# A fused attention and two feed-forward layers on one core: another order of the same 1776 steps

## The chip, the core and the metric

One core of one Trainium2 chip. The metric is the device time of one execution in microseconds (us), lower is better. The engines are TensorE (PE, its weight loads shown as PEld), VectorE (DVE), ScalarE (ACT), GpSimd (POOL) and SyncE (SP, which here only issues DMAs). Each engine runs its own instructions strictly in the order in which the program lists them.

## What is computed

```python
scores = scale * np.matmul(q, k.transpose(0, 1, 3, 2))        # 2 x 12 heads, 448 x 448, head size 64
scores = np.where(mask, -1000000000.0, scores)                # causal
attn = np.exp(scores - np.max(scores, axis=-1, keepdims=True))
attn = attn / (np.sum(attn, axis=-1, keepdims=True) + 1e-09)
x = np.matmul(attn, v)                                        # then laid out as 896 tokens x 768
h = x @ w_in; r = np.maximum(h, 0.0); x = (r * r) @ w_out     # 768 -> 2048 -> 768
h = np.maximum(np.maximum(x @ w1, x @ w2), x @ w3)            # three times 768 -> 768
return h @ w_o                                                # 768 -> 768
```

All inputs and outputs are float32.

## The kernel before

The work has two parts that overlap a little. First comes the attention, for 12 pairs of heads. Behind it come four products of the feed-forward layers, each done by Strassen-like sevens: seven products M1 to M7 of sums of halves instead of eight, with each operand split into a high and a low part so that three matmuls (high by high, low by high, high by low) make one product.

The order of everything is written out by hand in one string, ORDER (line 28), of 1776 step names. A loop at the end walks through it and calls each step, and each step issues its instructions at once, on the engines that it names. So ORDER fixes for every engine what stands behind what; only semaphores between the engines decide when something starts. After the string's end a fixed piece of code finishes the last product.

The steps of the attention, for pair number i (the number behind the dot): `s0`, `s2`, `s4`, `s6` are score matmuls on PE; `m0` to `m6` subtract, mask and find the extreme on DVE (line 474); `e0` to `e6` are the exponentials on ACT (482); `a0` to `a2` and `r0` to `r2` add the small constant and take the reciprocal of the sums (489, 493); `n0` to `n6` multiply by it (497; the tiles 0 and 1 are 128 wide, 2 and 3 are 256, 4 and 5 are 384, 6 is 448); `g0` to `g3` transpose on PE (508); `h0` to `h3` copy the transposed probabilities to where the last product wants them (521 for `h3`, 523 for the others: `h0` 768 wide, `h1` and `h3` 512, `h2` 256); `w0` to `w3` are the last product on PE (533), which needs all four `h` of its pair. `xf`, `xh`, `xl` copy the result out (540, 544, 203); `d1` to `d4`, `1h` to `4h` and `1l` to `4l` make sums of results and split them.

The steps of the layers: the block of weights `i4` is loaded by SP into one of two buffers, `C.i4` makes a cast of its upper half (264 or 267), `J.i4` joins the two halves on DVE (274) and issues the next load. `T1` to `T4` make the sums of weight blocks (213, on DVE; for `w_out` three of the four are accumulating DMAs that POOL issues, 210). `H.f0M6` casts the high part of the weights for product M6 of the seven f0 (200 on ACT, 290 on POOL), `L.f0M6` subtracts it to get the low part on DVE (203), `M6.f0` runs its 9 or 10 matmuls on PE (605), and `V0.f0M6` and so on read the result out of PSUM on ACT and DVE. Letters f, o and h stand for the three groups of sevens: w_in, w_out, and w1 to w3. The high and low parts lie in a ring of 5 buffers.

A step name with an apostrophe is the same step on another engine: `H'` and `C'` are POOL's in place of ACT's, `h'`, `xh'` and `xf'` DVE's in place of ACT's, `n'` DVE's in place of POOL's, `a'` POOL's in place of DVE's, `1h'` to `4h'` POOL's in place of ACT's. For blocks of w_out the apostrophe of `C'` has no effect.

```python
for n in ORDER.split():
    todo[n]()
    step, *i = n.split(".")
    if step == "s0" and int(i[0]) + 3 < B * NP:
        todo[f"load.{int(i[0]) + 3}"]()
```

Of the kernel before, what the change touches and what calls it, by code (L numbers as in the profile page):

```python
# [33 lines left out]
n3.1 n5.2 n2.1 e0.2 s4.3 e1.2 s2.3 g1.1 a2'.2 e3.2 n6.2 w1.0 m4.3 e1.3 n4.2 w2.0 e0.3 h1.1 a1'.2
m5.3 m2.3 m3.3 e4.3 r2.2 r1.2 n0.2 g3.1 m6.3 e5.3 a2'.3 h3.1 g0.2 g3.2 w3.0 n3'.2 h0.2 xh'.0 h3.2
xf'.0 n2.2 s6.4 r2.3 g1.2 s2.4 h1.2 e2.3 s0.4 n1.2 xl.0 e3.3 m2.4 a1'.3 m3.4 e6.3 a0'.3 g2.2 m1.4
h2.2 w0.1 e3.4 m6.4 m0.4 e2.4 s4.4 r1.3 n2'.3 s2.5 n3.3 a1'.4 r0.3 e6.4 m4.4 m5.4 n1.3 g1.3 w1.1
n0'.3 m2.5 m3.5 n6'.3 w2.1 w3.1 n5.3 e1.4 r1.4 e0.4 n4.3 e5.4 e4.4 a2'.4 e3.5 s6.5 g2.3 h1'.3
h2'.3 g3.3 m6.5 d3.1 h3.3 s4.5 g0.3 m4.5 s0.5 C'.i0 e2.5 h0.3 n2.4 w0.2 n3.4 a0'.4 3h'.1 w1.2 r2.4
m1.5 w2.2 r0.4 e6.5 e4.5 e1.5 m5.5 n0'.4 m0.5 n1.4 e0.5 a1.5 w3.2 n6.4 xf.2 r1.5 g1.4 g2.4 J.i0  # L40
n5.4 g3.4 s6.6 h1'.4 h2.4 s2.6 a2.5 n4.4 3l.1 r2.5 h3.4 m2.6 n2.5 e5.5 m3.6 xh.2 e2.6 a0'.5 xl.2
r0.5 s4.6 g0.4 n3.5 e3.6 a1'.6 h0.4 m5.6 e5.6 s0.6 m0.6 w0.3 m1.6 w1.3 w2.3 n6.5 w3.3 m4.6 n0.5
n1.5 g3.5 m6.6 e0.6 e1.6 r1.6 e6.6 d2.3 xh.3 g1.5 n5.5 h3'.5 g2.5 h2'.5 h1.5 s6.7 n4.5 m6.7 g0.5
e4.6 a2'.6 a0'.6 n3.6 xl.3 s2.7 d1.3 m3.7 h0.5 n2.6 e6.7 s4.7 s0.7 r0.6 C'.i2 1h.3 m2.7 m0.7 r2.6
m5.7 e3.7 e2.7 w0.4 w1.4 m1.7 n0.6 w2.4 w3.4 n1.6 e1.7 e5.7 a1'.7 n5.6 m4.7 d4.3 s0.8 g2.6 e4.7
xh.4 n4'.6 g1.6 xf.4 r1.7 a0'.7 h1.6 n6.6 s6.8 m1.8 e1.8 m0.8 s2.8 h2'.6 s4.8 r0.7 n6.7 1l.3 g3.6
m2.8 e0.8 m3.8 2h'.3 xl.4 g0.6 H'.f0M1 a2'.8 w0.5 e0.7 4h'.3 m4.8 w1.5 e2.8 e3.8 w2.5 h3.6 m5.8
n5'.7 w3.5 g3.7 n4'.7 s4.9 a2'.7 r2.7 a1.8 n3.7 m6.8 n1.7 e4.8 h0.6 r1.8 n2.7 g0.7 J.i2 h3.7 g1.7
d3.5 e6.8 m5.9 s6.9 w0.6 m4.9 e5.8 n0.7 h0.7 g2.7 m6.9 s2.9 3h'.5 h1.7 e4.9 2l.3 m2.9 H'.f1M2 e6.9
s0.9 w1.6 m3.9 w2.6 h2.7 H'.f1M1 a0'.8 3l.5 w3.6 n2.8 n3.8 g1.8 e5.9 r0.8 L.f1M2 xh.6 n6.8 a0.9  # L50
m0.9 s2.10 n4.8 m1.9 n5.8 s6.10 r2.8 s4.10 h1.8 r0.9 m3.10 xf.6 e3.9 xl.6 n6.9 C'.i1 n1.8 g0.8
# [6 lines left out]
T1.f0 h1.10 r2.11 a0'.11 r0.11 h0.10 2h.7 g3.10 w1.9 n4'.11 w2.9 w3.9 h3.10 n6'.11 n1.11 n5.11
e3.11 M2a.f0 n0'.11 g0.11 d3.9 g2.11 e2.11 w0.10 w1.10 T2.f0 a1.11 r1.11 w2.10 h0.11 C.i4 w3.10
4l.3 n2.11 h2'.11 g3.11 n3.11 3h.9 d4.7 H'.f0M6 2l.7 T3.f1 3l.9 h3.11 xh.10 g1.11 h1.11 xl.10  # L60
H'.f0M5 M2b.f0 xf.10 L.f0M6 J.i4 T3.f0 T4.f0 M1a.f1 M1b.f1 M1c.f1 1h'.7 1l.7 w0.11 C.i5 w1.11
4h'.7 w2.11 V0.f1M1 V0.f0M1 J.i5 w3.11 more 4l.7 d2.11 T2.f1 M2c.f0 H.f1M6 2h'.11 M2a.f1 M2b.f1
H'.f1M3 2l.11 M2c.f1 C.i7 L.f1M6 M6.f0 H.f0M7 L.f0M5 V0.f0M6 M6.f1 d1.11 J.i7 1h.11 H.f1M5 L.f0M7
C.i11 L.f1M5 wload d4.11 M7.f0 H.f1M7 xh.11 1l.11 V0.f0M7 H'.f0M4 T4.f1 4h.11 M5.f1 xl.11 T1.f2
V0.f1M6 V0.f0M2 M5.f0 L.f0M4 J.i11 C.i6 M4.f0 V1.f0M7 L.f1M7 M7.f1 H.f1M4 H.f2M1 J.i6 L.f2M1
V0.f0M4 T1.f3 H'.f0M3 H.f3M5 T2.f2 V0.f1M7 V0.f1M2 L.f0M3 L.f1M4 M1.f2 V1.f1M2 C.i10 L.f1M3 T2.f3
L.f3M5 M4.f1 H.f3M1 L.f3M1 V2.f0M7 V2.f1M2 V0.f1M4 V0.f2M1 4l.11 M3.f0 H'.f2M6 J.i10 C.i12 V1.f1M7
M1.f3 M3.f1 V0.f3M1 H'.f3M6 V3.f0M7 T3.f3 J.i12 T1.f5 H.f3M7 L.f3M6 H.f2M2 M6.f3 H.f3M2 C'.i13
L.f2M6 V0.f1M3 L.f2M2 M2.f2 T4.f2 L.f3M2 V0.f0M3 J.i13 V2.f1M7 C.i8 H'.f2M5 L.f2M5 T3.f2 V0.f3M6
L.f3M7 T4.f3 M5.f3 M2.f3 V0.f3M2 M6.f2 H.f2M7 J.i8 T3.f5 H.f2M4 V0.f2M6 M7.f3 L.f2M7 L.f2M4 C'.i9  # L70
J.i9 H'.f3M4 M7.f2 V0.f3M7 L.f3M4 M5.f2 M4.f3 T1.f4 V0.f2M2 V1.f3M7 C'.o3l J.o3l H.f5M1 L.f5M1
T1.f6 T2.f6 V0.f2M7 H.f3M3 T2.f5 T3.f4 H'.f4M1 L.f4M1 V1.f0M4 V0.f3M4 H.f5M6 XH.o1M1 C.i15 M4.f2
V1.f2M7 V0.f2M4 T2.f4 L.f5M6 H'.f2M3 M1.f5 L.f3M3 V3.f1M7 V0.f5M1 V2.f2M7 M1.f4 L.f2M3 H'.f4M6
L.f4M6 V0.f4M1 J.i15 M3.f2 H.f4M2 L.f4M2 C.i14 V0.f2M3 V1.f3M4 J.i14 H'.f5M5 V1.f2M4 M6.f4 T1.f7
H.f5M2 V1.f1M4 S3.o1 T4.f5 C'.o0l M6.f5 V0.f4M6 M2.f4 L.f5M2 H'.f4M7 J.o0l H'.f5M7 V1.f0M2 M2.f5
# [1180 lines left out]
```

## Time and profile before

| what | value |
|---|---|
| time, median of 3 runs | 445.79 us (444.44 to 446.27) |
| the profiled execution's own time | 446.14 us |
| its span | 444.4 us |
| granted TensorE clock, mean share | 0.999 |
| busy in the span: PE, DVE, ACT, POOL | 98%, 90%, 65%, 37% |

The span is the profiled execution from its first to its last instruction; its own time adds 1.7 us around that. The busy share of PE says little by itself, because matmuls overlap and their ends are modelled: it is the stretches of time that tell which engine sets the pace.

### The profile page before, as it was taken

How to read it: one execution, taken by the hardware profiler on the slowest of the kernel's cores; microseconds unless marked ns; L12 is line 12 of the kernel's file. 1: busy time of each engine (PE TensorE's matmuls, PEld its weight loads, DVE VectorE, ACT ScalarE, POOL GpSimd, SP SyncE). 2: the span in 40 equal slices, each digit the busy share in tenths (PEclk: the TensorE clock that was granted, in tenths of full speed). 3: DMA queues.
4: the chain of work that ended last, by engine and by line, in shares of the span. 5: the costliest groups of instructions: out<-in, count | busy, mean ns of one | idle time of the engine just before them, and what ended most of it. 6: DMA issues, size and time to landing. Idle time of an engine off the chain costs nothing.

```text
span 444.4 us, 7641 instructions
## 1 busy us (share of the span) xinstructions
...
## 2 busy tenths in 40 slices
...
GB/s 241 213 126 195 189 174 113 135 165 189 164 139 210 140 143 147 227 192 214 149 90 153 248 75 142 71 143 71 164 121 214 144 140 3 0 1 0 45 45 160
DMA packets 42854, 61.04 MB, mean 137 GB/s; under 512 B 2112, under 2 KB 35008, under 8 KB 42816
## 3 DMA queue, kind: packets, MB, share of 16 engines
...
q14 instruction: 18, 0.15, 0.1%
...
## 4 chain that ended last, share of the span: by engine, by line
PE 47%; DVE 2%; DMA 2%; ACT 0%; issue 0%
PE ps L605 38%; PE ps L1045 7%; DMA wr<-in_moe_w 2%; PE ps L1152 1%; DVE wd L274 0%; DVE g L213 0%; DVE wq L203 0%; DVE y L213 0%; ACT up L264 0%; DVE s L213 0%; DVE x L834 0%; ACT wq L200 0%; ACT x L827 0%; ACT y L887 0%; DVE x L203 0%
## 5 line engine op out<-in xcount | busy, mean ns | idle before, releaser
L605 PE MATMUL ps<-s,wq 128*128 128x448 f32 (+1 forms) x629 | 130.4, 361 | 0.0
L605 PEld LDWEIGHTS ps<-s,wq 128*128 128x128 f32 x629 | 115.5, 188 | 9.6 <-DVE s L203 0.4
L605 PE MATMUL ps<-x,wq 128*128 128x448 f32 (+1 forms) x518 | 104.6, 362 | 0.6 <-DVE wq L203 0.4
L605 PEld LDWEIGHTS ps<-x,wq 128*128 128x128 f32 x518 | 94.6, 188 | 9.9 <-DVE wq L203 1.6
L605 PE MATMUL ps<-a,wq 128*128 128x448 f32 x459 | 99.5, 367 | 0.0
L605 PEld LDWEIGHTS ps<-a,wq 128*128 128x128 f32 x459 | 86.0, 188 | 7.3 <-issue 0.3
L290 POOL CAST wq<-wd 128x384 fp32r<-128x384 f32 x43 | 46.9, 1092 | 85.9 <-PE ps L605 82.8
L203 DVE TENSOR_TENSOR wq<-wd,wq 128x384 fp32r<-128x384 f32 x99 | 57.4, 593 | 5.6 <-POOL wq L290 3.0
L274 DVE SCALAR_TENSOR_TENSOR wd<-wr,up 128x768 int32<-128x768 int32 x56 | 56.0, 999 | 6.3 <-ACT up L267 2.5
L290 POOL CAST wq<-wt 128x384 fp32r<-128x384 f32 x35 | 28.0, 801 | 88.9 <-PE ps L605 71.2
L482 ACT ACTIVATE pr<-pr,st 128x256 f32<-128x256 f32 (+3 forms) x84 | 44.0, 532 | 3.7 <-DVE st L474 3.0
L203 DVE TENSOR_TENSOR wq<-wt,wq 128x384 fp32r<-128x384 f32 x68 | 39.4, 588 | 7.3 <-POOL wq L290 6.3
L264 ACT CAST up<-wr 128x768 f16<-128x768 bf16 x28 | 30.3, 1081 | 21.4 <-DVE wd L274 15.9
L497 POOL TENSOR_SCALAR pr<-pr,st 128x128 f32<-128x128 f32 (+3 forms) x68 | 40.7, 611 | 8.5 <-DVE st L493 6.1
L200 ACT CAST wq<-wd 128x384 fp32r<-128x384 f32 x56 | 28.5, 511 | 19.1 <-PE ps L605 17.8
L200 ACT CAST wq<-wt 128x384 fp32r<-128x384 f32 x33 | 16.8, 511 | 22.7 <-PE ps L605 18.9
L474 DVE CUSTOM_DVE_ANT_0 pr<-pp,mask 128x256 f32<-128x256 f32 (+2 forms) x72 | 27.5, 413 | 4.2 <-PE pp L463 3.9
L639 ACT COPY s<-ps 128x448 f32<-128x448 f32 x38 | 20.0, 530 | 16.5 <-PE ps L605 16.5
L508 PEld LDWEIGHTS pp<-ident,pr 64*128 64x128 f32 x384 | 15.4, 138 | 14.2 <-POOL pr L497 5.8
L203 DVE TENSOR_TENSOR x<-g,x 128x448 fp32r<-128x448 f32 x40 | 25.2, 645 | 1.4 <-ACT x L200 1.4
L200 ACT CAST x<-g 128x448 fp32r<-128x448 f32 x40 | 22.1, 563 | 5.3 <-PE ps L605 2.5
L533 PE MATMUL ps<-ph,v 128*64 128x448 f32 (+3 forms) x192 | 24.5, 389 | 0.1
...
## 6 DMA issues: line engine op xcount, KB each, us to landing
...
```

Source lines behind the costliest of these rows:

```text
L200: nc.scalar.copy(hi, src)
L203: nc.vector.tensor_tensor(out=lo, in0=src, in1=hi.bitcast(F32), op=SUB)
L264: copy(self.up.bitcast(FH)[:, :, 1::2], self.top)
L274: nc.vector.scalar_tensor_tensor(out=self.t.bitcast(I32), in0=self.rest, scalar=13, in1=self.up.bitcast(I32), op0=ALU.logical_shift_right, ...
L290: copy(self.t[:, 0], self.src())
L474: nc.vector.tensor_tensor_reduce(out=self.pr[:, offs[u]:offs[u] + n], in0=self.sc[u][:, :n], in1=mask[:, mask.shape[1] - n:], scale=-SCALE ...
L482: nc.scalar.activation(sl, sl, ACTF.Exp, bias=self.st[:, 0, u:u + 1], scale=-1.0, accum_out=self.st[:, 1, u:u + 1],)
L497: engine.tensor_scalar(sl, sl, self.st[:, 2, u:u + 1], 1.0, op0=ALU.mult, op1=ALU.mult)
L533: nc.tensor.matmul(self.pv[r, kc * P:], self.n["v"][:, kc, r], self.ph[:, h, at], start=kc == 0, stop=kc == NK - 1,)
L605: nc.tensor.matmul(acc[:, c], w, x[:, c], skip_group_check=True, **flags)
L639: nc.scalar.copy(self.s[n], self.b)
L1045: nc.tensor.matmul(acc, a, b, start=start and i == 0 and e == 0, stop=i == KH - 1 and e == 2, skip_group_check=True,)
```

## The change

The string ORDER is replaced by another order of the same steps. Ahead of the apostrophes the two lists hold the same 1776 names. 161 steps change their engine: among them 49 casts `H` go from POOL to ACT and 30 the other way, so that POOL has 61 of them now instead of 80; DVE has 13 of the 48 copies `h` of the placed probabilities, not 10 (three more `h1`, one more `h3`, one less `h2`), 18 products `n` for 16 (eleven 128 wide, not five; two 384 wide, not five; one 448 wide, not two), 11 additions `a` for 10, and no `xf` for 1. The two calls that start a load ahead of its turn (`wload`) stand elsewhere: the first stood in pair 0 and stands in pair 1, the second stood behind `C.i11` and stands behind `L.f7M7`. The new string is one line shorter, so every later line number is less by one. Nothing else is touched.

```diff
 ORDER = """
-s2.0 m2.0 m3.0 s0.0 m1.0 e2.0 s4.0 m0.0 e3.0 e0.0 m4.0 s6.0 e1.0 a1'.0 s2.1 wload e4.0 s0.1 m5.0
+s2.0 s0.0 m2.0 s4.0 m0.0 m1.0 s6.0 e2.0 e1.0 m3.0 m4.0 s2.1 e3.0 m5.0 s0.1 m6.0 a1'.0 e4.0 e5.0
...
```

DVE at the end of the attention, ahead of the first product that needs a sum of weights. Before, from the reciprocal of pair 11 (`r1.11`, on st_1080) over the copy `h2'.11` (ph_1255) to `L.f0M6`, the last row:

```order
L493 RECIPROCAL st_1080<-st_1080 128x2
L203 TENSOR_TENSOR s4_827<-s_748,s4_827 128x448
L523 COPY ph_1255<-pp4_73 128x2x2x64
L213 TENSOR_TENSOR s_1274<-s_966,s_1076 128x448
L203 TENSOR_TENSOR s2_1195<-s_1076,s2_1195 128x448
L213 TENSOR_TENSOR wt_1279<-wd_1123 128x384
L203 TENSOR_TENSOR s3_1272<-s_1239,s3_1272 128x448
L203 TENSOR_TENSOR a12_1283<-ps7_69,a12_1283 128x448
L203 TENSOR_TENSOR wq_1276<-wt_1188,wq_1276 128x384
```

Now, from behind the copy `h1'.11` to the same `L.f0M6` (wq_1294, the last row):

```order
L273 SCALAR_TENSOR_TENSOR wd_1289<-wr_1134,up_64 128x768
L212 TENSOR_TENSOR wt_1311<-wd_983 128x384
L202 TENSOR_TENSOR s2_1097<-s_1032,s2_1097 128x448
L202 TENSOR_TENSOR a12_1300<-ps7_69,a12_1300 128x448
L212 TENSOR_TENSOR wt_1311<-wd_537,wt_1198 128x384
L212 TENSOR_TENSOR wt_1339<-wd_1132 128x384
L273 SCALAR_TENSOR_TENSOR wd_1341<-wr_1291,up_64 128x768
L202 TENSOR_TENSOR wq_1322<-wt_1311,wq_1322 128x384
L202 TENSOR_TENSOR s1_1155<-s_1091,s1_1155 128x448
L202 TENSOR_TENSOR s4_1336<-s_1201,s4_1336 128x448
L212 TENSOR_TENSOR s_1362<-ps7_69,s_1218 128x448
L202 TENSOR_TENSOR wq_1294<-wt_1198,wq_1294 128x384
```

Between the last copy of a placed probability and `L.f0M6` stood 5 instructions on DVE, and 11 stand there now. In all of DVE's program ahead of `L.f0M6` the steps outside the attention proper are eight more: two joins `J`, three sums `T`, one `L`, one sum `d` and, net, one `l`.

PE at the same place. Before, the last product of pair 10 ends (ps7_69, first row), 16 transposes of pair 11 follow, 12 matmuls of M2.f0 and M1.f1, the last product of pair 11, 12 matmuls more, and M6.f0 (wq_1276):

```order
L533 MATMUL ps7_69<-ph_1171,v_1102 64x64 x2
L508 MATMUL pp2_77<-ident_90,pr1_109 128x64 x8
...
L605 MATMUL ps0_1221<-a12_946,wq_1150 128x448 x3
L605 MATMUL ps2_1314<-a11_391,wq_927 128x448 x3
...
L533 MATMUL ps7_69<-ph_1255,v_1154 64x448 x2
...
L605 MATMUL ps0_1221<-a12_1283,wq_1150 128x448 x3
L605 MATMUL ps3_1315<-a12_600,wq_916 128x448 x3
...
L605 MATMUL ps6_68<-s2_804,wq_1276 128x448 x3
```

Now (M6.f0 is wq_1294):

```order
L532 MATMUL ps7_69<-ph_1153,v_1080 64x448 x2
L507 MATMUL pp2_77<-ident_90,pr1_109 128x64 x8
L507 MATMUL pp4_73<-ident_90,pr1_109 128x64 x4
L532 MATMUL ps7_69<-ph_1153,v_1080 64x320 x2
...
L604 MATMUL ps2_1306<-a11_348,wq_826 128x448 x3
...
L532 MATMUL ps7_69<-ph_1266,v_1164 64x448 x2
...
L604 MATMUL ps3_1307<-a12_1300,wq_800 128x448 x3
L604 MATMUL ps0_1224<-a12_1300,wq_1043 128x448 x3
L604 MATMUL ps6_68<-s2_696,wq_1294 128x448 x3
```

The transposes now stand inside pair 10's last product; 30 matmuls of the layer stand ahead of pair 11's last product instead of 24, and 6 behind it instead of 12. Ahead of M6.f0 there are 36 in both.

## Rows read from the trace of the kernel before

**Rows 1.** Busy time by stretch: engine busy (instructions), clock, DMA share, GB/s.

```profile
60.00:80.00 20.00, 18.13 (x198) 12.04 (x195) 19.51 (x61) 17.46 (x48) 15.23 (x25) 1.00 0.39 111
95.00:215.00 120.00, 120.00 (x601) 110.89 (x600) 107.41 (x184) 92.63 (x190) 41.40 (x43) 1.00 0.66 175
```

Behind the stretch's length the busy times stand in this order: PE, PEld, DVE, ACT, POOL.

**Rows 2.** Timeline of PE, 78 to 93 us: start, length, what.

```profile
78.80 2.69 PE L605 MATMUL ps<-a,wq 128*128 128x448 f32 x12
81.42 1.95 PE L533 MATMUL ps<-ph,v 128*64 128x448 f32 x16
...
85.84 7.38 PE L605 MATMUL ps<-s,wq 128*128 128x448 f32 x35
```

**Rows 3.** Timeline of DVE, 74 to 87 us, around the end of the attention.

```profile
76.67 0.42 DVE L523 COPY ph<-pp 128x256 f32<-128x256 f32 x1
...
80.12 0.83 DVE L203 TENSOR_TENSOR wq<-wt,wq 128x384 fp32r<-128x384 f32 x1
```

**Rows 4.** Groups on DVE, 0 to 95 us: count, busy, mean ns, idle before.

```profile
L274 DVE SCALAR_TENSOR_TENSOR wd<-wr,up 128x768 int32<-128x768 int32 x8 | 8.3, 1035 | 0.0
L203 DVE TENSOR_TENSOR s<-s,s 128x448 fp32r<-128x448 f32 x11 | 7.5, 686 | 0.5 <-POOL s L559 0.5
...
L203 DVE TENSOR_TENSOR wq<-wt,wq 128x384 fp32r<-128x384 f32 x6 | 3.4, 593 | 0.0
L213 DVE TENSOR_TENSOR wt<-wd 128x384 f32<-128x384 f32 x5 | 3.3, 654 | 0.0
...
L497 DVE TENSOR_SCALAR pr<-pr,st 128x384 f32<-128x384 f32 x5 | 2.5, 521 | 0.0
L213 DVE TENSOR_TENSOR wt<-wd,wt 128x384 f32<-128x384 f32 x4 | 2.2, 547 | 0.0
L523 DVE COPY ph<-pp 128x256 f32<-128x256 f32 x5 | 2.1, 416 | 0.2 <-PE pp L508 0.2
...
L489 DVE TENSOR_SCALAR st<-st 128x2 f32<-128x2 f32 x8 | 1.9, 253 | 0.1
L213 DVE TENSOR_TENSOR s<-ps,s 128x448 f32<-128x448 f32 x3 | 1.9, 617 | 0.0
...
L497 DVE TENSOR_SCALAR pr<-pr,st 128x128 f32<-128x128 f32 x5 | 1.8, 366 | 0.0
...
L521 DVE COPY ph<-pp 128x512 f32<-128x512 f32 x2 | 1.4, 683 | 0.0
L523 DVE COPY ph<-pp 128x512 f32<-128x512 f32 x2 | 1.3, 672 | 0.0
L497 DVE TENSOR_SCALAR pr<-pr,st 128x448 f32<-128x448 f32 x2 | 1.2, 616 | 0.0
...
L540 DVE COPY s<-ps 128x448 f32<-128x448 f32 x1 | 0.6, 615 | 0.0
```

**Rows 5.** Waits of DVE, 0 to 95 us: total us, times, longest.

```profile
DVE pr L474 <- PE pp L463: 3.9, 4, 3.1
...
DVE ph L523 <- PE pp L508: 0.7, 2, 0.5
```

**Rows 6.** Waits of PE's weight loads, 90 to 400 us: total us, times, longest.

```profile
PEld ps L605 <- DVE wq L203: 1.8, 5, 0.8
PEld ps L605 <- ACT y L887: 0.6, 1, 0.6
```

**Rows 7.** Timeline of all engines, 56 to 61 us.

```profile
58.80 1.06 POOL L264 CAST up<-wr 128x768 f16<-128x768 bf16 x1
...
58.84 1.38 DVE L203 TENSOR_TENSOR wq<-wd,wq 128x384 fp32r<-128x384 f32 x1
```

**Rows 8.** Casts of weights on POOL and on ACT, groups of the whole span.

```profile
L290 POOL CAST wq<-wd 128x384 fp32r<-128x384 f32 x43 | 46.9, 1092 | 85.9 <-PE ps L605 82.8 <-DVE wq L203 3.1
L200 ACT CAST wq<-wd 128x384 fp32r<-128x384 f32 x56 | 28.5, 511 | 19.1 <-PE ps L605 17.8 <-ACT x L200 0.7 <-issue 0.4
```

**Rows 9.** What SP's queue waits for, whole span: total us, times, longest.

```profile
SPq L251 <- DVE wd L274: 258.5, 51, 16.4
```

More of the change, by code (lines that the diff above doesn't have):

```diff
@@ L34 @@
[L34 to L51, printed above, removed]
@@ L58 @@
[L58 to L75, printed above, removed]
@@ L142 @@
[L142 to L146 removed]
+s2.0 s0.0 m2.0 s4.0 m0.0 m1.0 s6.0 e2.0 e1.0 m3.0 m4.0 s2.1 e3.0 m5.0 s0.1 m6.0 a1'.0 e4.0 e5.0
+e6.0 m2.1 m0.1 m1.1 e0.1 m3.1 r1.0 s6.1 s4.1 a0'.0 r0.0 n3.0 e0.0 e1.1 n6.0 m6.1 e2.1 a2.0 n5.0
@@ new lines @@
+e4.10 w2.8 h3.9 d1.7 w3.8 h0.9 a0.10 2h.7 g1.9 e6.11 e1.10 r0.10 xf.8 n4.10 m4.11 n5.10 xh.8 m5.11
+M1a.f0 n2.10 M1b.f0 g2.9 h1'.9 h2.9 e0.10 J.i3 g0.10 s2.11 xl.8 L.f0M2 e5.11 h0.10 1h'.7 m3.11
+a2'.10 r2.10 s0.11 w0.9 m0.11 n6.10 e4.11 e0.11 w1.9 m2.11 m1.11 g3.10 g1.10 a0.11 e1.11 h1.10
+w2.9 w3.9 n1.10 T1.f0 r0.11 d4.7 a2'.11 n0'.10 e3.11 h3.10 n4.11 e2.11 n5'.11 M1c.f0 g2.10 r2.11
+d3.9 M2a.f0 n6'.11 M2b.f0 n1'.11 h2.10 a1'.11 T1.f1 r1.11 n3'.11 3h'.9 T2.f1 n2.11 n0'.11 g0.11
+g3.11 C.i4 h0.11 T2.f0 w0.10 h3.11 g1.11 g2.11 w1.10 V0.f0M1 h1'.11 J.i4 h2.11 H.f0M6 w2.10 w3.10
@@ new lines @@
+xh.10 M1a.f1 T3.f0 M1b.f1 M2a.f1 M1c.f1 H'.f0M7 2l.7 xf.10 xl.10 C.i5 V0.f1M1 M2b.f1 w0.11 4h.7
+T4.f0 T3.f1 J.i5 H.f1M6 w1.11 w2.11 L.f0M7 1l.7 4l.7 w3.11 M2c.f1 M2c.f0 d2.11 H'.f0M5 L.f0M6
+2h.11 more C.i7 2l.11 L.f1M6 H.f1M5 xh.11 d1.11 d4.11 M6.f0 3l.9 L.f0M5 J.i7 V0.f0M6 1h.11 H.f0M4
+M6.f1 M7.f0 4h.11 C.i11 T1.f2 1l.11 M5.f0 L.f1M5 xl.11 J.i11 T4.f1 L.f0M4 H.f0M3 M5.f1 H.f1M7
+L.f0M3 V0.f1M6 H.f2M1 C'.i6 L.f1M7 V0.f0M7 M4.f0 V0.f0M2 T3.f2 V1.f0M7 L.f2M1 V0.f0M4 T2.f2 J.i6
+H.f1M4 T3.f3 V2.f0M7 C.i10 H.f2M6 M7.f1 H.f2M2 4l.11 M1.f2 L.f2M6 L.f2M2 L.f1M4 V0.f1M7 V0.f1M2
@@ new lines @@
+V0.f2M1 J.i10 H.f3M1 V3.f0M7 T1.f3 M3.f0 V1.f1M7 H.f2M7 M4.f1 L.f2M7 M2.f2 L.f3M1 V0.f1M4 H.f1M3
+M6.f2 L.f1M3 C'.i12 V0.f2M6 J.i12 M3.f1 V2.f1M7 M1.f3 T2.f3 H.f2M3 T3.f5 M7.f2 V0.f0M3 H.f2M5
+H'.f3M6 C.i9 V1.f1M2 J.i9 H.f3M2 V0.f3M1 V0.f2M7 V1.f1M4 L.f2M5 L.f3M6 C'.i8 V0.f1M3 M6.f3 H'.f3M7
+T4.f2 M5.f2 J.i8 V1.f0M4 T4.f3 V0.f3M6 L.f3M7 H'.f4M2 V2.f1M2 M7.f3 H.f2M4 T1.f4 L.f2M4 M4.f2
+L.f2M3 C.i13 XH.o1M1 V1.f0M2 V0.f2M4 T3.f4 V1.f2M7 H'.f3M5 T2.f4 J.i13 V2.f0M2 V2.f2M7 H'.f4M1
+L.f3M5 S3.o0 V1.f2M4 L.f3M2 M3.f2 L.f4M2 M5.f3 V0.f3M7 L.f4M1 H.f3M4 C'.i15 M2.f3 H'.f5M2 V0.f2M3
@@ new lines @@
+L.f6M4 H.f7M7 M5.f6 XL.o0M1 M5.f7 H.f6M3 V0.f6M7 H.o0M2 V1.f6M2 M4.f6 S2.o0 XH.o0M2 V1.f6M7 L.f6M3
+V0.f7M2 XL.o0M2 XH.o3M2 C.o0r V2.f5M7 H.o1M1 L.f7M7 wload S4.o0 M3.f6 L.o0M2 M7.f7 V0.f6M3 XH.o2M2
+V0.f6M4 J.o0r S1.o0 XH.o5M1 XL.o2M1 V0.f7M7 V1.f7M7 H.f7M4 M2.o0 H'.o0M1 C'.o1r V1.f6M3 V1.f6M4
+XH.o6M1 L.o0M1 V3.f5M7 L.o1M1 J.o1r H'.o3M2 XL.o3M2 M2.o1 XH.o1M4 V1.f4M3 M1.o0 XH.o3M6 S1.o3
+V2.f4M3 T1.o0 S4.o1 H'.f7M3 T1.o1 L.f7M4 M1.o1 XL.o5M1 S2.o5 M4.f7 V2.f4M7 S4.o3 H.o2M1 S1.o2
+V2.f6M7 L.f7M3 C'.o2r J.o2r H'.o2M2 M3.f7 XH.o1M6 H.o3M1 XH.o4M2 L.o2M1 V2.f6M3 H.o4M1 L.o2M2
```

172 lines of the change are left out of this document (91 added, 81 removed).

## The prediction

> **What bounds the kernel now.** I began with the busy times by stretch, because a busy share over the whole span hides that this kernel has two halves. From 95 us on TensorE has no gap: in the 120 us from 95 to 215 it is busy for all 120.00, with 601 matmuls, 200 ns apart, while DVE has 107 us of work, ACT 93 and POOL 41 [rows 1]. The clock stands at 1.00 there and ahead of it [rows 1], so no change of order can win or lose anything by the clock that these rows would show. Between 60 and 80 us it is otherwise: PE is busy 18.13 of 20 us with transposes and small matmuls, and DVE 19.51 [rows 1]. There DVE is the full engine, and ACT (17.46) and POOL (15.23) have some room.
>
> So I read the waits next, to see what the second half can still yield. PE's weight loads wait 1.8 us for low parts from DVE and 0.6 us for ACT between 90 and 400 us [rows 6], 2.4 us in all. A better order of the second half can win that and no more, since its matmuls are the same ones at the same spacing. What is left is **when the dense run of matmuls begins**, and whether it is broken once it has begun.
>
> That place is in the timelines. PE runs 12 matmuls of the layers from 78.80 us, the last product of pair 11 at 81.42, 12 more, and reaches M6.f0 at 85.84 [rows 2]. M6.f0 needs the low part of its weights, and DVE makes that at 80.12 for 0.83 us, so it is there at 80.95 [rows 3]. **PE comes 4.9 us behind DVE** at this product. I take this lead as the quantity to watch: the number of layer matmuls ahead of M6.f0 is 36 in both programs, so PE would come at 85.84 again, and whatever DVE gets in addition ahead of `L.f0M6` is paid from the 4.9 us first.
>
> **What the change adds on DVE ahead of L.f0M6.** I took the set of steps that DVE's program holds ahead of `L.f0M6` in each order and priced the differences with the mean durations of the groups up to 95 us [rows 4].
>
> Steps of the attention that change engine:
> - copies `h`: three more of 512 (L523) at 0.672 and one more at L521 at 0.683, one of 256 less at 0.416: 2.016 + 0.683 - 0.416 = +2.28 us
> - products `n`: six more of 128 at 0.366, three fewer of 384 at 0.521, one fewer of 448 at 0.616: 2.20 - 1.56 - 0.62 = +0.02 us
> - one copy `xf` less, 0.615, and one addition `a` more, 0.253: -0.36 us
>
> That is +1.9 us. The same copies leave ACT and small products leave and join POOL, but both have room at 60 to 80 us [rows 1], so what they gain there is worth nothing while DVE is the full engine.
>
> Steps of the layers that now stand ahead of `L.f0M6` and stood behind it: two joins at 1.035, three sums of weights (one at 0.654, two at 0.547), one `L` at 0.593, one `l` at 0.686 and one `d` at 0.617. 2.07 + 1.75 + 0.59 + 0.69 + 0.62 = +5.7 us.
>
> Durations overlap a little from one instruction to the next. From the copy at 76.67 to `L.f0M6` at 80.12 DVE starts six instructions in 3.45 us, and the durations of the six in the same timeline, the first of them 0.42, add up to 3.93 [rows 3]: 3.45 / 3.93 = 0.88. Then DVE comes (1.9 + 5.7) x 0.88 = 6.7 us later to `L.f0M6`, **6.7 - 4.9 = 1.8 us later than PE wants it**.
>
> Part of this is taken up by DVE's own idle time. Up to 95 us it waits 3.9 us for scores, of which 3.1 are the start, so 0.8; 0.7 for transposes [rows 5]; and 0.5 for POOL at an `l` [rows 4]. That makes 2.0 us which more work could fill. Only idle time that lies behind an added step's place, and that the new order doesn't make anew, is filled; no row says which share that is. The ends are 0 and 2.0. I take 0.6, nearest to the one wait that stands close to the attention's end (0.5 for POOL), since the others fall where PE and DVE take turns and another order brings its own. The gap is then 1.8 - 0.6 = 1.2 us; its bounds are 0 (all 2.0 filled) and 2.7 (nothing filled, durations not overlapping: 7.6 - 4.9).
>
> A gap here is not won back, because behind it PE has no other slack: it runs without a break from then on [rows 1].
>
> **The rest of the change.** POOL casts 61 weights instead of 80, and ACT 19 more. A cast takes 1.09 us on POOL and 0.51 on ACT, and both groups idle mostly for PE to give a buffer back (82.8 us and 17.8 us) [rows 8], so the cover of the 19 casts is ACT's free time: 19 x 0.51 = 9.7 us against 120 - 93 = 27 us in one stretch alone [rows 1]. I price it at nothing. Without that cover, one cast in the way costs 0.51 us. PE's waits for low parts (1.8) [rows 6] may shrink or grow by it; I leave them as they are. The two moved load calls pass joins, casts and other loads on SP's queue, which is never the late one: its loads wait 258.5 us in 51 waits for DVE's joins to free a buffer [rows 9]. The moved loads are behind the same joins and cost nothing; if that cover went, a block would come late once, by at most some tenths of the longest wait there.
>
> **A rule that speaks for a gain.** A join's cast on POOL began at 58.80 us, and an `L` that began at 58.84 on DVE took 1.38 us [rows 7], against 0.593 for the other group of `L` [rows 4]: 0.8 us more. The Trainium skill, page "SBUF — State Buffer", section "Who interferes with whom", states that a DVE instruction with two SBUF inputs and a GpSimd instruction that reads SBUF use one port pair and exclude each other for the whole instruction. By that rule these two would lie one behind the other, and the trace agrees as far as one pair shows. By the rule 19 fewer casts on POOL would give DVE time back, by the rows they give none that reaches PE, since PE sets the pace from 95 us on. The sum above is without it; it is rival D.
>
> **The sum.** Profiled time 446.14 + 1.2 = 447.3 us. The profiled execution is 0.35 us above the median of the runs (446.14 against 445.79), so the forecast for the median is 447.3 - 0.35 = **447.0 us**. With the bounds 0 and 2.7 it is 445.8 to 448.5.
>
> **Rivals.**
> - **A, the forecast**: DVE's lead is used up, a short break ahead of M6.f0 or just behind. 447.0, own range 445.8 to 448.0. Chance 0.40.
> - **B, slower, 448.9**: the dense run breaks twice. Nothing of the waits is filled (2.7 late), and the next product that needs a new low part finds DVE still behind by another 0.4, the value of nearly one more `L` (0.593 x 0.88 = 0.5): 445.8 + 2.7 + 0.4 = 448.9. Place: DVE from `r1.11` to `L.f0M4`. It decides as soon as DVE waits in the first 95 us more than it does now. For it: 12 instructions in one row on DVE ahead of `L.f0M6`, of which only the last is what PE waits for. Against it: all 2.0 us of waits would have to stay. Chance 0.27.
> - **C, no change, 445.4**: the added work fills the waits, lead and gap come out even, and a little of the 2.4 us of later waits goes (0.4): 445.8 - 0.4. This is also the case in which PE alone sets the time, and no order matters. For it: PE's 120.00 of 120. Against it: the full DVE. Chance 0.15.
> - **D, faster, 442.9**: the gap does not come, because DVE runs faster than its old durations. Four meetings of an `L` with a cast of POOL fewer, each 0.8 us [rows 7, 4], give 3.2 us, more than the 1.8; and PE's later waits, 2.4 [rows 6], go, with 0.5 us more from an earlier start: 445.8 - 2.4 - 0.5 = 442.9. For it: POOL loses work ahead of the dense run and behind it. Against it: up to M6.f0 POOL loses hardly more than three casts. Chance 0.18.
>
> **How the numbers follow.** A measurement of this kernel can tell about 0.5% from no change, 2.2 us here: faster is below 443.6, slower above 448.0. A lies within (0.35 of its 0.40, its upper end outside with 0.05), C lies within (0.15), B is slower (0.27), and D is faster (0.18). Same 0.50, slower 0.32, faster 0.18. The range must leave out 0.2: I cut D's fast half (below 443.2, some 0.10) and the slow tail of B above 450.0 (0.10), where a third break would have to come. Range 443.2 to 450.0.
>
> **What would show it.** In the changed kernel's trace: PE idle for about a microsecond just ahead of M6.f0, with its weight load waiting for DVE's low part there; `L.f0M6` some 6 us behind its old 80.12, and DVE's row of 12 instructions without a gap ahead of it; from 95 us on PE busy without a break again; POOL with 61 casts and PE not waiting for them. B would show a second wait of that kind within 10 us, and DVE's waits up to 95 us above today's 2.0 without the start. D would show M6.f0 at 85.8 or earlier, a mean duration of DVE's `L` and `T` below today's, and PE's waits from 90 to 400 us under 1 us. I am wrong altogether if the end of the attention moves by more than 3 us in either direction, because then an engine other than DVE sets it.

## The result, and the profile after

The changed kernel takes 449.98 us (median of 6 executions, 448.31 to 451.6) against 445.73 us for the kernel before (444.44 to 446.27): a ratio of 1.0099, with a 95% interval of 1.0072 to 1.0126. It is about 1% slower. The forecast was 447.0 with no change that can be told as the likeliest outcome; the time lies at the upper edge of the range (443.2 to 450.0), on the side of the rival "slower" (448.9). But the mechanism was neither the forecast's nor that rival's, as the trace shows at once. The profiled execution took 450.09 us, with a span of 448.3 us.

The busy times by stretch answer to [rows 1]; the columns are the stretch, then PE, PEld, DVE, ACT, POOL busy with their instructions, the granted clock, DMA share and GB/s. After:

```profile
60.00:80.00 20.00, 19.78 (x206) 13.06 (x203) 19.20 (x65) 18.72 (x50) 14.01 (x24) 1.00 0.36 107
95.00:215.00 120.00, 116.47 (x572) 107.62 (x572) 103.19 (x175) 86.94 (x182) 33.15 (x41) 0.97 0.63 167
```

Between 60 and 80 us PE is busier than before (19.78 for 18.13): the end of the attention got better. From 95 to 215 us PE has 3.5 us less to show than the 120.00 of [rows 1], and the clock is no longer 1.00. The loss lies in the half on which the prediction spent one paragraph.

The place where the prediction looked, PE's timeline from 78 us, answers to [rows 2] (start, length, what):

```profile
78.58 3.36 PE L604 MATMUL ps<-a,wq 128*128 128x448 f32 x15
81.87 1.95 PE L532 MATMUL ps<-ph,v 128*64 128x448 f32 x16
83.75 1.49 PE L604 MATMUL ps<-a,wq 128*128 128x448 f32 x6
85.07 8.10 PE L604 MATMUL ps<-s,wq 128*128 128x448 f32 x41
```

M6.f0 starts at 85.07, 0.8 us earlier than the 85.84 of [rows 2], with nothing idle ahead of it. Its low part, `L.f0M6`, stands in DVE's timeline, which answers to [rows 3]:

```profile
84.40 0.55 DVE L202 TENSOR_TENSOR wq<-wt,wq 128x384 fp32r<-128x384 f32 x1
```

It ends at 84.95, and 4.9 us of lead have become 0.1. The lead was indeed used up, and it was just enough.

What PE's weight loads wait for from 90 to 400 us answers to [rows 6]:

```profile
PEld ps L604 <- DVE wq L202: 4.7, 4, 3.9
```

Of 4.7 us, 3.9 are one single wait. PE's timeline from 200 us shows it, and DVE's and POOL's timelines show what stands there (behind a row, in brackets, the idle time before it and who ended it):

```profile
199.81 4.63 PE L604 MATMUL ps<-x,wq 128*128 128x448 f32 x23
207.97 8.37 PE L604 MATMUL ps<-x,wq 128*128 128x448 f32 x28 [3.53 <-DVE wq L202]
```

```profile
201.78 0.55 DVE L202 TENSOR_TENSOR wq<-s,wq 128x384 fp32r<-128x384 f32 x1
206.89 0.56 DVE L212 TENSOR_TENSOR s<-wd 128x384 f32<-128x384 f32 x1 [4.57 <-DMA wd<-wd]
207.36 0.55 DVE L202 TENSOR_TENSOR wq<-wd,wq 128x384 fp32r<-128x384 f32 x1
```

```profile
196.95 0.86 POOL L209 DMA_DIRECT2D wd<-wd  x1 [4.14 <-DMA wd<-wd]
197.48 1.21 POOL L209 DMA_DIRECT2D wd<-s  x1
198.02 1.56 POOL L209 DMA_DIRECT2D wd<-wd  x1
200.61 0.86 POOL L209 DMA_DIRECT2D wd<-wd  x1 [1.03 <-DVE wd L273]
```

By the steps' order these rows have names. On POOL: the accumulating DMAs T3.o2, T4.o0, T1.o5 and T1.o4. On DVE: L.o0M6, the sum T2.o5 at 206.89, and L.o5M2 at 207.36. T2.o5 reads the block into which T1.o5 accumulates, and T1.o5 was issued at 198.02 as the third of three DMAs within 1.1 us. DVE did nothing but stand in front of T2.o5 from 202.3 us. **L.o5M2 behind it needs nothing of T2.o5**; it is the low part that PE waits for at M2.o5. The chain of waits over this stretch (start, length, what) reads the same:

```profile
198.02 8.85 DMA wd<-wd
206.87 0.02 issue
206.89 0.56 DVE s L212
207.45 0.48 DVE wq L202
207.93 0.04 issue
207.97 8.17 PE ps L604 x27
```

And the break has a second price, in the clock. The stretches around it, in the columns of the first table:

```profile
204.40:208.00 3.60, 0.07 (x2) 0.03 (x1) 1.11 (x3) 0.65 (x2) 0.85 (x2) 0.84 0.89 248
208.00:210.00 2.00, 2.00 (x5) 1.79 (x6) 2.00 (x5) 0.53 (x1) 0.90 (x2) 0.50 0.72 115
210.00:212.00 2.00, 2.00 (x7) 1.78 (x6) 2.00 (x5) 1.01 (x3) 0.00 (x0) 0.50 0.51 81
212.00:214.00 2.00, 2.00 (x8) 1.78 (x7) 0.40 (x1) 1.80 (x5) 1.54 (x2) 0.58 0.06 10
214.00:216.00 2.00, 2.00 (x13) 1.86 (x12) 1.82 (x3) 0.03 (x1) 0.78 (x2) 1.00 1.06 164
```

PE stood still for 3.5 us and came back at a granted clock of 0.50, the lower of its two levels (1.2 GHz of 2.4), for over 5 us: the first nine matmuls behind the break took 3.73 us, and nine of that shape take 1.99 at a clock of 1.00. The first run below shows what break and clock cost together: 5.75 us.

### The profile page after: what moved, and what is told of

The parts are those of the page before. It is cut to its first block, busy times and chain, and to the rows that moved or that the text cites. A ratio compares the mean times of both kernels' runs of the same rounds, so it can differ in the third digit from the quotient of the medians.

```text
span 448.3 us, 7631 instructions
## 1 busy us (share of the span) xinstructions
PE 437.8 (98%) x2609; PEld 381.2 (85%) x2609; DVE 395.2 (88%) x853; ACT 292.8 (65%) x659; POOL 135.6 (30%) x208
## 4 chain that ended last, share of the span: by engine, by line
PE 88%; DVE 4%; DMA 3%; ACT 3%; issue 1%; POOL 1%; DVEq 0%
PE ps L604 69%; PE ps L1044 7%; PE ps L532 4%; DMA wd<-wd 3%; PE pp L507 2%; PE pp L462 2%; ACT pr L481 2%; DVE pr L473 2%; PE ps L1151 1%; PE ps L453 1%; PE ps L1118 1%; DVE st L488 0%; DVE ph L522 0%; DVE s L202 0%; ACT ph L522 0%
## 5 line engine op out<-in xcount | busy, mean ns | idle before, releaser
L604 PE MATMUL ps<-x,wq 128*128 128x448 f32 (+1 forms) x518 | 106.4, 367 | 3.5 <-DVE wq L202 3.5
L604 PEld LDWEIGHTS ps<-x,wq 128*128 128x128 f32 x518 | 97.2, 193 | 12.1 <-DVE wq L202 4.4
L273 DVE SCALAR_TENSOR_TENSOR wd<-wr,up 128x768 int32<-128x768 int32 x56 | 54.5, 974 | 9.5 <-ACT up L266 3.8
L289 POOL CAST wq<-wd 128x384 fp32r<-128x384 f32 x34 | 27.8, 818 | 80.1 <-PE ps L604 76.1
L289 POOL CAST wq<-wt 128x384 fp32r<-128x384 f32 x27 | 19.4, 719 | 103.0 <-PE ps L604 78.5
L202 DVE TENSOR_TENSOR wq<-wt,wq 128x384 fp32r<-128x384 f32 x68 | 40.9, 608 | 9.8 <-POOL wq L289 6.2
L199 ACT CAST wq<-wd 128x384 fp32r<-128x384 f32 x65 | 32.9, 511 | 24.9 <-PE ps L604 22.2
L496 POOL TENSOR_SCALAR pr<-pr,st 128x256 f32<-128x256 f32 (+3 forms) x66 | 38.3, 592 | 5.4 <-DVE st L492 2.6
L199 ACT CAST wq<-wt 128x384 fp32r<-128x384 f32 x41 | 20.9, 512 | 10.4 <-PE ps L604 9.9
L462 PE MATMUL pp<-k,q 64*128 64x256 f32 (+2 forms) x144 | 23.6, 427 | 0.5 <-DVE st L473 0.3
```

Of the source, the lines that this page charges most:

```text
L199: nc.scalar.copy(hi, src)
L202: nc.vector.tensor_tensor(out=lo, in0=src, in1=hi.bitcast(F32), op=SUB)
L273: nc.vector.scalar_tensor_tensor(out=self.t.bitcast(I32), in0=self.rest, scalar=13, in1=self.up.bitcast(I32), op0=ALU.logical_shift_right, ...
L289: copy(self.t[:, 0], self.src())
L462: nc.tensor.matmul(self.sc[w][:, :keys[w]], self.n["q"][r, w // 2 * P:(w // 2 + 1) * P], self.n["k"][r, :keys[w]], start=True, stop=True,)
L496: engine.tensor_scalar(sl, sl, self.st[:, 2, u:u + 1], 1.0, op0=ALU.mult, op1=ALU.mult)
```

## The experiments

Each run edits the string ORDER alone. "Before" in the same batch took 445.36 us (e1 to e4), 445.97 (e5 to e8), 445.42 (e9 to e11) and 445.96 (e12).

### One step moved on DVE

```diff
 # order of the changed kernel
-... H.o7M2 XH.o2M5 T2.o5 L.o5M2 ... L.o7M2 V2.oM1 T2.o4 T2.o2 ...
+... H.o7M2 XH.o2M5 L.o5M2 ... L.o7M2 T2.o5 V2.oM1 T2.o4 T2.o2 ...
```

> The changed order with one step moved: the sum T2.o5 on DVE goes from ahead of L.o5M2 to behind L.o7M2. Theory (a step at the wrong place): T2.o5 waits on DVE for the accumulating DMA of T1.o5, and L.o5M2, which needs nothing of it, stands behind it in DVE's queue and keeps M2.o5 waiting. Then PE's break of 3.5 us at 204 us and the lower clock behind it go, and the time is 449.98 - 3.5 - 2.7 = 443.8 us. Rival (the DMAs are late whatever stands there): the break moves to the next sum that reads an accumulated block, T2.o4 or T2.o2, and the time stays at 448 to 450 us.

Measured: 444.23 us, ratio 0.9973 to before (0.9960 to 0.9985). One step, moved by twelve places, is worth 5.75 us (5.6 by the two ratios to before), and the kernel is now a little faster than the kernel before. PE's row from 95 to 215 us and DVE's row at T2.o5:

```profile
95.00:215.00 120.00, 120.00 (x604) 111.31 (x603) 108.69 (x185) 90.49 (x190) 32.18 (x42) 1.00 0.64 173
```

```profile
206.86 0.56 DVE L212 TENSOR_TENSOR s<-wd 128x384 f32<-128x384 f32 x1 [0.42 <-DMA wd<-wd]
```

PE has its 120.00 back and the clock its 1.00. T2.o5 starts at 206.86 as against 206.89, so the DMA was as late as ever; but DVE now stands in front of it for only 0.42 us, and PE not at all. The rival (the break moves on to the next sum) is out.

### The DMA's place in POOL's queue

T2.o5 stays ahead of L.o5M2 here. What changes is which place T1.o5 has among the three accumulating DMAs: first (e3) or second (e11), where the changed kernel has it third.

```diff
 # e3
-... T3.o2 J.o5r V2.f7M3 S2.o4 XL.o7M1 T4.o0 ... H.o1M6 T1.o5 ...
+... J.o5r T1.o5 V2.f7M3 S2.o4 XL.o7M1 T4.o0 T3.o2 ... H.o1M6 ...
 # e11
-... T3.o2 J.o5r V2.f7M3 S2.o4 XL.o7M1 T4.o0 ... H.o1M6 T1.o5 ...
+... T3.o2 J.o5r V2.f7M3 S2.o4 XL.o7M1 ... H.o1M6 T1.o5 T4.o0 ...
```

> The changed order with T2.o5 left where it is, but on POOL the accumulating DMA T1.o5 issued ahead of T4.o0 and T3.o2, right behind the join J.o5r that it needs. If it is POOL's own queue that makes T1.o5 late (two accumulations of 192 KB ahead of it), it lands 2 us or more earlier, the break shrinks below 1.5 us, and the time is 444.5 to 447 us. If the weight loads on the same 16 engines make it late, it lands at most 1 us earlier, a break of 2.5 us or more stays, and the time is 448.5 to 450 us.

> The changed order, T2.o5 at its place, with one thing moved on POOL: T4.o0 behind T1.o5, so that T1.o5 is the second of the three accumulating DMAs and not the third (third: landed 8.9 us after its issue, time 449.98; first: landed about 5.8 us after, 444.3). If each accumulation ahead of it in POOL's queue delays it by its own transfer, it lands 7 to 7.5 us after its issue, the break is 1.5 to 2.5 us, and the time with the slower clock is 445.5 to 448 us. If only being first helps, 449 to 450 us; if being third is what hurts, 444.3 us.

Measured: 444.3 us as the first (ratio 0.9969, 0.9956 to 0.9982) and 445.68 us as the second (1.0006, 0.9990 to 1.0021). DVE's row at T2.o5 as the first, then as the second:

```profile
203.42 0.56 DVE L212 TENSOR_TENSOR s<-wd 128x384 f32<-128x384 f32 x1 [0.62 <-DMA wd<-wd]
```

```profile
205.10 0.56 DVE L212 TENSOR_TENSOR s<-wd 128x384 f32<-128x384 f32 x1 [2.38 <-DMA wd<-wd]
```

T1.o5 is issued at 197.61 as the first, 197.76 as the second and 198.02 us as the third, and T2.o5 starts 5.8, 7.3 and 8.9 us after that. **At this place every accumulation ahead of it costs 1.5 us.** The loads of weights do not make this difference: SP issues the two that are near at 196.9 to 197.3 and 200.3 to 200.8 us in all three. But neither 1.5 us nor 5.8 us is a fixed price. Below is the time from issue to landing (the last number, us) of T1.o5 in before and in e2 (further down), where the accumulation before it was issued 3.8 us earlier, and of an accumulation that the changed kernel issues at 207.15, when the weights have all but landed:

```profile
wd<-wd POOLq DMA_DIRECT2D x1, 192.0 KB, 4.4
wd<-wd POOLq DMA_DIRECT2D x1, 192.0 KB, 6.1
wd<-wd POOLq DMA_DIRECT2D x1, 192.0 KB, 3.0
```

The next one behind that last one lands 3.7 us after its issue, only 0.7 more. What else is under way at the time has a share in the delay that no run here separates.

The first place came out nearly as expected (444.3 us for 444.5 to 447). As the second, PE's break is 1.33 us, a little less than the 1.5 to 2.5 expected, and the clock stays at 1.00:

```profile
206.18 6.14 PE L604 MATMUL ps<-x,wq 128*128 128x448 f32 x29 [1.33 <-DVE wq L202]
```

```profile
205.50:208.00 2.50, 1.82 (x9) 1.61 (x9) 2.50 (x6) 0.64 (x2) 1.60 (x2) 1.00 1.11 294
```

So from first to second the 1.3 us break costs 1.4 us of time, and from second to third 2.2 us more of break cost 4.3. The difference of 2 us is what the clock adds. The matmuls themselves give somewhat more: 15 of them start 0.37 us apart behind the break and 0.20 apart from 213.7 us on, 15 x 0.17 = 2.6 us.

### The same break made in the old order

```diff
 # order of before; e2
-... H'.o1M6 L.o5M2 XH.o6M2 ... M2.o5 T2.o5 T2.o4 ...
+... H'.o1M6 T2.o5 L.o5M2 XH.o6M2 ... M2.o5 T2.o4 ...
 # e12: e2, and on POOL
-... T2.o2 T1.o5 M1.o5 T4.o2 ...
+... T2.o2 M1.o5 T4.o2 T1.o5 ...
```

> The order of before with one step moved the other way: T2.o5 directly ahead of L.o5M2 on DVE. Theory: DVE then stands at T2.o5 from 204.3 us until the DMA of T1.o5 (issued at 198.3) has landed; if that takes 8.9 us as in the changed kernel, L.o5M2 ends at about 208.3 instead of 204.8, PE breaks for 2 to 3 us ahead of M2.o5 (due 205.66), and the clock falls: 448 to 451 us. Rival (in the old order the DMA lands in about 5 us, so only the changed order's crowd of DMAs makes the wait): no break, 445.5 to 446 us.

> The order of before with both conditions of the break made: T2.o5 directly ahead of L.o5M2 on DVE (alone it cost nothing, 445.94 us) and the accumulating DMA T1.o5 issued behind T4.o2 instead of ahead of it on POOL (issue at about 200.1 us instead of 197.9). Theory (landing is 5.8 us as the first, 1.5 us more for each accumulation ahead of it): T1.o5 lands at about 207.4, DVE stands at T2.o5 for 3 us, PE breaks for 2 to 3 us ahead of M2.o5, 447.5 to 451 us depending on whether the clock falls. Rival (the break belongs to the changed order's other steps): no wait of PE above 1 us, 445 to 446.5 us.

Measured: 445.94 us for e2 (1.0003, 0.9989 to 1.0017), so my expectation for it was a miss: it took over the 8.9 us of a third DMA, and here no other accumulation stands close ahead of T1.o5. It was issued at 197.91 and DVE had to wait 0.18 us for it before 204.15. With T4.o2 ahead of it as well: 448.94 us (1.0079, 1.0048 to 1.0110). DVE's row at T2.o5 in e2, then in e12:

```profile
204.15 0.56 DVE L213 TENSOR_TENSOR s<-wd 128x384 f32<-128x384 f32 x1 [0.18 <-DMA wd<-wd]
```

```profile
206.08 0.56 DVE L213 TENSOR_TENSOR s<-wd 128x384 f32<-128x384 f32 x1 [2.01 <-DMA wd<-wd]
```

In e12 T1.o5 is issued at 199.38 and used 6.7 us later, less than the 7.3 of a second place, and PE's break is 1.36 us, not the 2 to 3 that I expected. T2.o5 starts 1.93 us later than in e2; 1.47 of that are the later issue, and only 0.46 can be the place behind T4.o2. The profiled execution, with the clock at 1.00, took 447.5 us; the others, three of them with a clock of 0.992 to 0.996, 448.8 to 451.4. The break needs both: an accumulation that lands late, and the sum ahead of the low part. In the changed order it is the place in POOL's queue that makes it late (e3, e11), in e12 mostly the later issue. The old order has neither, and both can be put into it.

### Both repairs

```diff
 # order of the changed kernel: T2.o5 as in e1, T1.o5 as in e3
```

> The changed order with both repairs: T2.o5 behind L.o7M2 on DVE, and T1.o5 ahead of T4.o0 and T3.o2 on POOL. Either alone took the break away, so both should give the same 443.8 to 444.5 us; if what is left of DVE's waits for accumulating DMAs (1.0 to 1.2 us) reached PE, up to 1 us less, 443.2.

Measured: 443.84 us, ratio 0.9957 (0.9942 to 0.9971): the fastest of all, though not to be told from e1 and e3. Without its one break the new order is worth 0.3 to 0.4%.

### Who does what in the attention

These runs test the ledger, the +1.9 us of DVE work that the prediction charged for steps changing their engine.

```diff
 # e4: order of before; 60 attention steps on the engines of the changed kernel
 # e7, e9, e10: order of before; of these 60 the copies (16), the additions (17), the products (22) alone
 # (the other 5, sums of results, were not tried alone)
-... h2.1 ... a1.1 ... n4.0 ...
+... h2'.1 ... a1'.1 ... n4'.0 ...
 # e5: the order of e1; the same 60 steps on the engines of before
```

> The order of before, with every attention step on the engine that the changed kernel gives it (60 steps, the h, n, a, xf, xh and the h-sums), nothing else. The prediction's ledger says DVE gets 1.9 us more work by this: the lead of 4.9 us at M6.f0 falls to about 3, the time stays within 445.0 to 446.5 us. Rival (the ledger is worth something because DVE is full): the end of the attention moves back by 1 to 2 us and the time is 446.7 to 447.7 us. Other rival (POOL and ACT were late in places where nobody saw it): the end moves forward by about 1 us, 444.5 to 445.

> The order of before with only the copies h, xf and xh on the engines of the changed kernel (16 steps), a part of the 60 that together cost 8.5 us. By the ledger DVE gets 2.28 - 0.62 = 1.7 us more. If DVE's sum of work is what cost the 8.5 us, this run costs 1.5 to 3 us: 447 to 448.5 us. If the cost lies in the additions and products that POOL got (DVE waited 4.3 us in 5 places for POOL's additions), it is 445 to 446.5 us.

> The order of before with only the additions a on the engines of the changed kernel (17 steps, nine from POOL to DVE and eight from DVE to POOL): the second part of the 60 that together cost 8.5 us. If DVE's waits for POOL's additions (4.3 us in the run with all 60) are what these cost, this run is slower by 3 to 5 us: 449 to 451 us. If the additions wait only because POOL's products stand ahead of them, it is within 1 us of before: 445 to 447 us.

> The order of before with only the products n on the engines of the changed kernel (22 steps), the third part. By the ledger DVE's work is the same (0.02 us): 445.5 to 446.5 us. If an engine that gets a product at a place where it is needed soon holds up PE's transposes or its own queue, 448 us or more. The three parts together should come near the 8.5 us of all 60: 1.3 for the copies, and 7 for these two runs.

> The changed order with T2.o5 moved as in the run before (444.2 us), and the attention steps back on the engines of before (60 steps). Theory (engines and order of the attention were chosen for one another; what counts is where an in-order engine meets a step that isn't ready): slower by 3 us or more, 447 us and up, with new waits of DVE, ACT or POOL up to 95 us. Rival (the ledger: DVE's work is what counts, and it has 1.9 us less now): faster, 442.5 to 443.5 us.

Measured:

| run | time, us | ratio to before (95%) | the ledger's price, us | M6.f0 starts, us | lead, us |
|---|---|---|---|---|---|
| e4, all 60 | 453.90 | 1.0191 (1.0170 to 1.0212) | +1.9 | 92.85 | 4.6 |
| e7, copies | 447.30 | 1.0034 (1.0017 to 1.0051) | +1.7 | 87.56 | 5.2 |
| e9, additions | 451.39 | 1.0133 (1.0107 to 1.0158) | +0.25 | 91.87 | 4.9 |
| e10, products | 449.98 | 1.0102 (1.0064 to 1.0140) | 0.0 | 89.55 | 4.6 |
| e5, new order, old engines | 452.27 | 1.0121 (1.0093 to 1.0150) | -1.9 from 444.2 | 93.45 | 0.1 |

The last two columns are read from the timelines: when M6.f0 starts on PE, and how far ahead of that `L.f0M6` ends on DVE. In before they are 85.84 and 4.9, in e1 85.16 and 0.1.

None of the three expectations for e4 held: the highest of them ended at 447.7 us. The copies cost 1.3 us (0.8 to 2.3 by the interval) for a price of 1.7. By the prediction the lead of 4.9 us should have paid for them, and it did not. PE's row at M6.f0 and DVE's row at `L.f0M6` in e7, for the 85.84 and 80.12 of [rows 2] and [rows 3]:

```profile
87.56 9.41 PE L605 MATMUL ps<-s,wq 128*128 128x448 f32 x47
81.76 0.57 DVE L203 TENSOR_TENSOR wq<-wt,wq 128x384 fp32r<-128x384 f32 x1
```

PE comes 1.7 us later and DVE 1.6, so the lead stays. In every run of the table M6.f0 moves by about what the run costs. **Where attention steps get slower, PE and DVE come later together, and the lead pays nothing.**

The additions cost 6.0 us for a price of 0.25, and the products 4.6 for nothing. Part of what the additions cost shows in DVE's waits up to 95 us (total, times, longest) of e9:

```profile
DVE pr L474 <- PE pp L463: 5.2, 6, 3.1
DVE st L493 <- POOL st L489: 3.3, 3, 2.4
```

and in PE's waits of the same run up to 110 us, which in before are 1.4 us in 3 times:

```profile
PE pp L508 <- POOL pr L497: 3.0, 6, 0.9
```

At the longest of the three, DVE stands in front of a reciprocal for 2.4 us until POOL has done an addition of 0.2 us that lies behind other work in POOL's queue; before had no such wait, and e10 has 3.1 us of it. So the expectation that additions wait only because of the moved products is out: they do it alone. The three parts add up to 11.9 us, and all 60 steps together cost 8.5, so the parts hide each other to some extent. e5 is the counterpart: with less work for DVE, the new order loses 8 us. DVE's waits up to 95 us in e5:

```profile
DVE pr L473 <- PE pp L462: 5.8, 7, 3.1
DVE s L212 <- ACT a L543: 2.7, 2, 1.4
```

Old order with old engines 445.4, new order with new engines 444.2; either crossed, 452 to 454. The engines of the attention steps belong to their order.

### The casts

```diff
 # order of e1; 101 casts H and C on the engines of before
-... H.o0M6 ...
+... H'.o0M6 ...
```

> The same base (444.2 us), and the casts H and C of all weights back on the engines of before, 80 H on POOL again instead of 61. Theory (the prediction's price of nothing: both engines idle for PE): 443.5 to 445.2 us, no further break of PE above 1 us. Rival (a cast on POOL holds up DVE's instructions with two inputs in SBUF): DVE's mean duration of L rises by 20 ns or more, DVE ends later in several places, PE's waits for low parts rise by 1.5 us or more and the time is above 446 us.

Measured: 453.38 us (1.0159, 1.0138 to 1.0180), 9.2 us more than its base. The price of nothing was expected to hold and did not. The rival had the time right (above 446 us), but its reason is far too small. DVE's two groups of L in e6, then in e1 (count, busy, mean ns, idle before):

```profile
L202 DVE TENSOR_TENSOR wq<-wd,wq 128x384 fp32r<-128x384 f32 x99 | 57.8, 595 | 11.4 <-ACT wq L199 6.0 <-POOL wq L289 5.2
L202 DVE TENSOR_TENSOR wq<-wt,wq 128x384 fp32r<-128x384 f32 x68 | 39.3, 587 | 6.4 <-ACT wq L199 4.0 <-POOL wq L289 2.4
```

```profile
L202 DVE TENSOR_TENSOR wq<-wd,wq 128x384 fp32r<-128x384 f32 x99 | 56.4, 580 | 6.5 <-POOL wq L289 4.5 <-ACT wq L199 2.1
L202 DVE TENSOR_TENSOR wq<-wt,wq 128x384 fp32r<-128x384 f32 x68 | 41.1, 610 | 9.6 <-POOL wq L289 5.9 <-ACT wq L199 3.7
```

Nineteen more casts on POOL make one group 15 ns longer and the other 23 ns shorter, 0.1 us in all. These means hide what happens to single instructions. Sort all L by whether a cast or a product of POOL runs at the same time in the trace. In e1 the 132 L without one take 550 ns, none more than 561, and the 43 with one take 716, up to 1372. In e6 it is 548 ns (118 of them) and 682 (57). DVE's sums with one input from PSUM do not show it (in e1 603 ns without and 612 with). So POOL's work does hold up L, by 7.2 us in all in e1; but the 19 more casts bring 14 more meetings and only 0.4 us more.

M6.f0 starts at 85.90, 0.7 us later than in e1. The rest are waits of PE's weight loads, spread over the whole second half; in e1 they are 1.5 us for DVE's low parts (4 times, longest 0.6) and 0.6 us of issue. In e6, from 90 us on:

```profile
PEld ps L604 <- DVE wq L202: 4.7, 11, 1.3
PEld ps L604 <- issue: 2.1, 1, 2.1
PEld ps L604 <- ACT wq L199: 1.5, 1, 1.5
PEld ps L604 <- POOL wq L289: 1.2, 1, 1.2
```

Which of the 101 casts cost most was not tried.

## Why the prediction was wrong

That the time fell inside the range, and near rival B's, is luck: none of the terms that make up the range is the one that cost the time.

**The bound** was read rightly: e1 gives PE its 120.00 us of 120 back. "PE has no gap from 95 us on" was a reading of the old order, though, and the sum used it for the new one.

**The part "the rest of the change" is the step that failed.** It names SP's queue, ACT and POOL's casts, and prices all else at nothing. It leaves out POOL's accumulating DMAs and the sums on DVE that read them. The new string has the three T steps in a row on POOL, and T2.o5 directly ahead of L.o5M2. Standing there, T2.o5 cost 5.75 us (e1), all of the slowdown and more.

**The clock.** That "no change of order can win or lose anything by the clock that these rows would show" was wrong as it was used, since the rows were those of the old order: the break was followed by 0.50, and the clock made up 2 to 2.6 us of the loss. In the Trainium skill, the page "TensorE: Matmul & The Clock Gate", Part 1 on the clock gate, gives two levels for a busy and for an idle array; the trace agrees, with 1.00 ahead of the break of 3.5 us and 0.50 behind it, and 1.00 all through the break of 1.33 us.

**The sum at M6.f0** has a second step that failed: it let the lead of 4.9 us pay for the attention's +1.9 us as well, on the ground that "PE would come at 85.84 again". In the old order the lead stays at 4.6 to 5.2 us whichever engines the attention steps have (e4, e7, e9, e10), and in the new order it is 0.1 with the new engines (e1) and with the old (e5). So the lead went with the new order, not with the engines. The layer steps that now stand ahead of `L.f0M6`, 5.7 x 0.88 = 5.0 us by the prediction's own price, fit the 4.8 us that went, and without the attention's share the sum has hardly a gap (5.0 - 4.9). That is an inference: no run moves these layer steps alone.

The sizes were off too. Instead of 6.1 us (6.7 less 0.6 of waits) DVE came 4.3 us later to `L.f0M6` (84.40 for 80.12), and PE came 0.8 us earlier instead of at the same time. The stretches up to `L.f0M6`, before and after, in the columns of the first table:

```profile
0.00:80.12 80.12, 76.35 (x780) 46.03 (x781) 73.05 (x281) 72.22 (x222) 59.31 (x122) 1.00 0.55 174
0.00:84.40 84.40, 81.55 (x811) 49.72 (x812) 78.33 (x293) 75.75 (x228) 57.93 (x117) 1.00 0.57 176
```

DVE's busy time grew by 5.3 us where 6.7 were charged, and its idle time shrank by 1.0 where 0.6 were taken off. The 0.6 was modelled on the wait of 0.5 for POOL, but in the kernel before that wait stands at 86.06 to 86.51 us, behind `L.f0M6`, where it could take up nothing:

```profile
86.51 0.89 DVE L203 TENSOR_TENSOR s<-s,s 128x448 fp32r<-128x448 f32 x1 [0.45 <-POOL s L559]
```

What went is the waits for scores: of the 3.9 us of [rows 5] only the start is left. And the durations were those of the old neighbours: L takes 552 ns now for the 593 of [rows 4]. After, up to 95 us:

```profile
DVE pr L473 <- PE pp L462: 3.1, 1, 3.1
```

```profile
L202 DVE TENSOR_TENSOR wq<-wt,wq 128x384 fp32r<-128x384 f32 x7 | 3.9, 552 | 0.0
```

The sums T say less: 654 in [rows 4] and 550 here, but 626 in e1 and 670 in e11, whose programs are the same up to there.

**The ledger** has about the right size for the copies (e7: 1.3 us measured, 1.7 charged), and its totals do not tell what a change of engine does in a crowded stretch (e9, e10).

**The rivals.** B had the right sign and almost the time, from the wrong place: DVE did not wait more up to 95 us, but less. D had the right signs for what the rest of the order does: M6.f0 earlier than 85.8, shorter L, and PE's later waits small, 0.8 us beside the one long wait. With the break repaired, 443.84 us, against D's 442.9. Its reason, fewer meetings with POOL's casts, exists but is small. Before, 53 L ran beside a cast or a product of POOL and took 683 ns, the 122 others 550; now it is 45 at 693 ns and 130 at 552. The time lost by it fell from 7.0 to 6.4 us in all. In the Trainium skill, the page "SBUF — State Buffer", section "Who interferes with whom", says that a DVE instruction with two inputs in SBUF contends with a GpSimd instruction that reads SBUF; the traces agree, with the 552 and 693 ns.

**What was right of the signs**: 61 casts on POOL with PE not waiting for them, DVE's row ahead of `L.f0M6` without a gap. **Open**: which casts cost e6 its 9 us, and how much of an accumulation's way is due to the loads beside it. For L up to 95 us the shorter mean is two instructions of 1.38 and 0.83 us that ran beside POOL's work before.
